# Casts of one batch's values cut into blocks of rows, and the order of all steps written anew, in a fused attention and highway kernel

## The chip, the core and the metric

The kernel runs on one core of a Trainium2 chip. A core has a matrix engine (TensorE, PE in the profile, with its weight loads as PEld), three engines for elementwise work (VectorE or DVE, ScalarE or ACT, GpSimd or POOL), and a fifth, SyncE or SP, whose queue issues nearly all DMAs here. They run at the same time and wait for each other through semaphores; each works off its own instructions in program order. The metric is the time of one execution on the device in microseconds.

## What is computed

An attention without a softmax over scores, and a highway layer over its result. Batch 8, 8 heads, 576 rows, 64 columns a head; all in float32 from and to memory.

```
q_s = exp(q) / sum over a head's columns          k_s = exp(k) / sum over the rows
kv  = k_s^T @ v            (64 x 64 for each batch and head)
x   = q_s @ kv             (4608 rows of 8 * 64 = 512)
H   = max(x @ w_h, 0)      T = sigmoid(x @ w_t + b_t)
out = T * H + (1 - T) * x
```

## The kernel before

The rows are worked off in 36 tiles of 128 rows. Two batches make nine tiles: four of the first, four of the second, one mixed. So tiles 0 to 3 and 4 to 7 belong to batches 0 and 1 and tile 8 to both; tiles 27 to 30, 31 to 34 and 35 belong to batches 6 and 7.

Nothing is scheduled by a compiler. The string ORDER (L16 to L63) lists some 700 steps, and the loop at L502 issues them one after the other. A step is named by its kind and its place, with an engine after a colon: `vc_1_2:A` casts slab 2 of batch 1's values on ACT. The order of the list is the order of each engine's own instructions, and so also of the DMA queue. Steps for a batch: `q`, `k`, `v` load (SP); `ek`, `eq` take the exponential into f16 (ACT); `vc` casts v into f16 (L258); `kv` is the product of k and v with an extra column of ones for the sums (PE, L264); `kr` and `kn` divide by the sums and keep the result (DVE); `qt` and `qc` turn q by TensorE and copy it out of PSUM; for batch 7 `qd` turns it by DMA. Steps for a tile: `xu` multiplies q with kv (PE), `rs` and `x` divide (DVE), `xt` and `xe` turn x and copy it (PE, then DVE or ACT), `mh` and `mt` are the products with the two weights (PE, L421 and L413, four of 512 columns each), `bw` puts the bias into the PSUM tile of mt (ACT), `th` is the tanh (ACT), `dd` and `uu` make the gated difference (DVE, or with `:P` two operations on POOL, "lifted", L451), `oo` adds x (POOL, L473), `st` stores (SP). `fill` are products of zeros that keep TensorE running in the first 15 us while the first loads arrive.

What ties the steps together beside the data are the buffers, which are used in turn:

- Loads of k, of v and of q have three buffers each; a load waits until the batch three before has been read.
- x in f16 has six buffers (`xp`): `x` of a tile waits for `oo` of the sixth tile before it in order.
- The outputs of two neighbouring tiles share one of seven buffers named o32 (the four halves of the weights pass through them first), so `oo` waits until the stores of the pair seven buffers before have landed. The mixed tiles and the last ones have three buffers of their own (o1).
- The products xu of a whole tile and kv share one PSUM tile (`ps_x`), so each waits until the one before has been read by DVE. The turned x has one PSUM tile, the turned q one, gate and H two each.
- d, u, tanh and the sums have three buffers each.

The cast is short:

```
def vc(e, b, c):
    n = 1 if b < 3 else 2
    copy = dict(A=nc.scalar.copy, D=nc.vector.tensor_copy, P=nc.gpsimd.tensor_copy)[e or "P"]
    copy(v16[b % NV][:, c:c + n, :, 0:D], T[f"v32{b}"][:, c:c + n].rearrange("p c (j d) -> p c j d", j=NJ))
```

A slab of batches 0 to 2 is 128 partitions by 9 blocks of 64, 576 elements a partition; without a letter the cast runs on POOL.

Of the kernel before, what the change touches and what calls it, by code (L numbers as in the profile page):

```python
# [16 lines left out]
setuppool q_0_0 v_0_0 fill_8 fill_8 b_32 b_0 eq_0_0 k_0_0 ek_0_0 qt_0_0 setupdve bsplit bp bc fill_8 ek_0_1 vc_0_0:D
v_0_1 vc_0_1 kv_0_0 kr_0_0 k_0_2 fill_8 ek_0_3 v_0_2 v_0_3 vc_0_2 qc_0_0 kn_0_0 xu_0_0 vc_0_3 ek_0_2 kv_0_1 kr_0_1
kn_0_1 q_0_4 fill_5 eq_0_1 eq_0_2 xu_1_0 rs_1_0 rs_0_0 x_1_0 x_0_0 fill_8 xt_1_0 xe_1_0:D qt_0_1 w_h_0 whd_1:P whd_0:P
whc_0:A qc_0_1 xt_0_0 xu_0_1 rs_0_1 x_0_1 bw_1 xe_0_0 xu_3_0 rs_3_0 x_3_0 qt_0_2 bw_0 w_h_2 whd_2:P whd_3:P whc_2:A  # L20
w_t_2 wtc_2:P xt_0_1 mh_0_0 xe_0_1:D xu_2_0 xt_3_0 xe_3_0 rs_2_0 w_t_0 wtc_0:P mh_1_0 q_1_0 mh_0_1 qc_0_2:A x_2_0
xt_2_0 dd_1 dd_0 k_1_2 eq_1_0 v_1_2 mt_1_0 th_1_0 uu_1_0 vc_1_3 oo_1_0 ek_1_2 ek_1_3 xe_2_0:D mt_0_1 mt_0_0 th_0_0
qt_1_0 qc_1_0 mh_3_0 bw_2 mt_2_0 vc_1_2:A kv_1_1 uu_0_0 oo_0_0 th_2_0 bw_3 mt_3_0 k_1_0 ek_1_1 ek_1_0 dd_3 kr_1_1
v_1_0 vc_1_0 vc_1_1:A kn_1_1 xu_5_1 th_3_0 rs_5_1 x_5_1 mh_2_0 dd_2 uu_2_0:P uu_3_0:P oo_2_0 oo_3_0 xt_5_1 xu_4_1
kv_1_0 kr_1_0 rs_4_1 bw_5 kn_1_0 xe_5_1 mt_5_1 x_4_1 q_1_4 eq_1_2 xu_5_0 rs_5_0 qt_1_2 qc_1_2 bw_4 xu_4_0 xu_8_0 x_5_0
eq_1_1 xt_5_0 qt_1_1 rs_4_0 x_4_0 mh_5_1 q_2_0 eq_2_0 k_2_2 rs_8_0 xe_5_0:D qc_1_1:A x_8_0 ek_2_3 xt_4_0 xt_4_1
xe_4_0:D xe_4_1:D mh_5_0 dd_5 mt_5_0 th_5_0 uu_5_0:P k_2_0 ek_2_1 bw_8:A ek_2_2 xu_6_0 rs_6_0 x_6_0 mt_4_1 xt_8_0
xe_8_0:D xu_6_1 rs_6_1 qt_2_0 x_6_1 xu_7_0 rs_7_0 x_7_0 mt_4_0 xt_6_0 xu_7_1 rs_7_1 xt_6_1 xe_6_0:D xe_6_1:D x_7_1
mt_8_0 ek_2_0 v_2_0 vc_2_0:D qc_2_0 mh_4_1 mh_4_0 xt_7_0 dd_4 xt_7_1 th_4_0 vc_2_1 kv_2_0 v_2_2 vc_2_3 vc_2_2:A kv_2_1
kr_2_1 mh_8_0 bw_6:A mh_6_1 th_8_0 mt_6_1 kr_2_0 oo_5_0 kn_2_1 uu_4_0:P kn_2_0 xu_9_0 dd_8 q_2_4 eq_2_2 eq_2_1 xe_7_1  # L30
uu_8_0:P oo_4_0 rs_9_0 x_9_0 mt_6_0 xe_7_0 qt_2_1 qc_2_1 th_6_0 mh_6_0 dd_6 mh_7_1 xt_9_0 xu_12_0 rs_12_0 x_12_0
uu_6_0:P oo_8_0 oo_6_0 xe_9_0:D mh_7_0 dd_7 bw_7:A mt_7_1 mt_7_0 xu_10_0 xt_12_0 mh_9_0 xe_12_0:D rs_10_0 q_3_0 x_10_0
eq_3_0 eq_3_1 qt_3_2 qc_3_2 dd_9 mh_12_0 xt_10_0 xe_10_0:D qt_3_1 qc_3_1 k_3_0 th_7_0 bw_10:A v_3_0 vc_3_0 xu_11_0
rs_11_0 bw_9:A mt_9_0 ek_3_0 ek_3_2 dd_12 vc_3_2:A x_11_0 qt_3_0 th_9_0 qc_3_0 uu_7_0:P oo_7_0 uu_9_0 mt_10_0 th_10_0
bw_12:A kv_3_0 qt_2_2 q_4_0 qc_2_2:A mh_10_0 eq_4_0:F kr_3_0 kn_3_0 xt_11_0 xe_11_0:D mt_12_0 dd_10 uu_10_0:P oo_9_0
oo_10_0 xu_14_0 rs_14_0 x_14_0 th_12_0 uu_12_0 oo_12_0 mh_11_0 qt_4_0 bw_11:A xu_13_0 rs_13_0 x_13_0 v_4_0 vc_4_0
xt_14_0 xe_14_0:D vc_4_2:A bw_14:A mt_11_0 th_11_0 xu_17_0 rs_17_0 x_17_0 qc_4_0:A xt_13_0 mh_14_0 dd_11 uu_11_0:P
oo_11_0 xu_15_0 rs_15_0 xe_13_0:D x_15_0 mt_14_0 dd_14 mh_13_0 xu_16_0 rs_16_0 x_16_0 bw_13:A xt_17_0 xe_17_0:D
mt_13_0 dd_13 k_4_0 ek_4_0 ek_4_2 q_4_9 kv_4_0 kr_4_0 kn_4_0 th_14_0 uu_14_0:P bw_17:A th_13_0 uu_13_0 xt_15_0 xe_15_0
qt_4_1 qc_4_1 mt_17_0 xu_18_0 rs_18_0 x_18_0 oo_14_0 q_5_0 eq_5_0 oo_13_0 v_5_0 vc_5_0 bw_15:A vc_5_2 mh_17_0 xt_16_0  # L40
xe_16_0:D dd_17 eq_4_2 eq_5_1 mt_15_0 th_15_0 xu_20_0 qt_4_2 k_5_0 rs_20_0 x_20_0 mh_15_0 th_17_0 uu_17_0:P oo_17_0
xt_18_0 mh_16_0 xu_19_0 dd_15 qc_4_2 xe_18_0:D rs_19_0 qt_5_0 qc_5_0 bw_16:A ek_5_0:F xt_20_0 x_19_0 q_6_0 xe_20_0:D
mt_16_0 th_16_0 bw_18:A qt_5_1 kv_5_0 eq_6_0:F dd_16 kr_5_0 kn_5_0 uu_16_0 bw_20:A xt_19_0 mh_18_0 qc_5_1:A st_1_0
st_1_1 mh_20_0 st_3_0 uu_15_0:P oo_15_0 xe_19_0:D xu_21_0 rs_21_0 x_21_0 oo_16_0 mt_18_0 th_18_0 k_6_0 st_3_1 v_6_0
mt_20_0 xu_22_0 dd_18 uu_18_0 oo_18_0 st_5_0 st_7_1 q_5_9 st_5_1 xt_21_0 rs_22_0 x_22_0 th_20_0 dd_20 uu_20_0:P
xe_21_0:D st_7_0 qt_6_0 mh_19_0 xu_23_0 rs_23_0 x_23_0 vc_6_2 dd_19 bw_19:A bw_21:A mt_19_0 ek_6_0 ek_6_2 mh_21_0
dd_21 xt_22_0 xe_22_0 xu_24_0 mt_21_0 mh_22_0 xt_23_0 rs_24_0 qc_6_0 x_24_0 vc_6_0:A kv_6_0 qt_6_1 th_19_0 uu_19_0:P
oo_20_0 q_6_9 dd_22 xe_23_0:D mh_23_0 kr_6_0 th_21_0 uu_21_0 oo_19_0 kn_6_0 bw_22:A mt_22_0 qc_6_1:A dd_23 xu_25_0
rs_25_0 x_25_0 eq_5_2 xt_24_0 qt_5_2 bw_23:A mt_23_0 th_22_0 oo_21_0 uu_22_0:P oo_22_0 qc_5_2:A xu_26_0 xe_24_0
rs_26_0 x_26_0 bw_24:A th_23_0 uu_23_0 xt_25_0 mh_24_0 dd_24 st_10_1 q_7_0 oo_23_0 v_7_0 st_10_0 vc_7_0 vc_7_2 k_7_0  # L50
mt_24_0 xe_25_0 eq_6_2 xu_27_0 qt_6_2 xt_26_0 mh_25_0 rs_27_0 x_27_0 xe_26_0:D xu_29_0 rs_29_0 bw_25:A mt_25_0 st_17_0
eq_7_0:F qd_7_0 qc_6_2:A dd_25 th_24_0 qd_7_1 x_29_0 xt_27_0 xe_27_0 uu_24_0 oo_24_0 mh_26_0 dd_26 xu_30_0 rs_30_0
th_25_0 x_30_0 st_12_0 uu_25_0:P mh_27_0 bw_27:A mt_27_0 st_14_1 dd_27 xt_30_0 xu_28_0 rs_28_0 q_7_9 st_12_1 bw_26:A
mt_26_0 st_14_0 st_23_0 st_16_0 st_16_1 xe_30_0:D mh_30_0 ek_7_0 oo_25_0 x_28_0 xt_28_0 xe_28_0:D ek_7_2 kv_7_0
xt_29_0 th_26_0 uu_26_0 oo_26_0 th_27_0 uu_27_0:P mh_28_0 bw_30:A mt_30_0 kr_7_0 kn_7_0 xu_31_0 st_21_0 bw_28:A
mt_28_0 dd_30 xe_29_0:D rs_31_0 dd_28 th_30_0 uu_30_0:P mh_29_0 x_31_0 xt_31_0 xe_31_0:D oo_27_0 oo_30_0 bw_29:A
xu_33_0 eq_7_2 th_28_0 rs_33_0 uu_28_0 mt_29_0 qt_7_2 bw_31:A mh_31_0 x_33_0 xt_33_0 xu_32_0 th_29_0 dd_29 rs_32_0
uu_29_0 qc_7_2:A oo_29_0 x_32_0 xe_33_0 mt_31_0 mh_33_0 xt_32_0 bw_33:A th_31_0 dd_31 st_8_0 st_19_0 st_26_0 xu_34_0
xe_32_0 uu_31_0 rs_34_0 mt_33_0 x_34_0 oo_28_0 st_28_0 st_30_0 oo_31_0 st_31_0 st_25_0 mh_32_0 xu_35_0 dd_33 xt_34_0
bw_32:A mt_32_0 th_33_0 uu_33_0:P oo_33_0 dd_32 xe_34_0:D mh_34_0 rs_35_0 x_35_0 xt_35_0 bw_34:A th_32_0 uu_32_0 dd_34  # L60
xe_35_0 mt_34_0 th_34_0 uu_34_0 oo_32_0 st_33_0 st_32_0 oo_34_0 st_34_0 bw_35_0 mh_35_0 dd_35 mt_35_0 th_35_0 uu_35_0
# [5 lines left out]
def kernel(  # L67
# [49 lines left out]
    spare = turned.rearrange("p a c d -> p (a c d)").bitcast(FP32)
    T = {}
# [136 lines left out]
        nc.scalar.activation(t[:, :, c:c + n].rearrange("p j c d -> p c j d"),  # L255
                             T[f"k32{b}"][:, c:c + n].rearrange("p c (j d) -> p c j d", j=NJ), AF.Exp)

    def vc(e, b, c):  # L258
        n = 1 if b < 3 else 2
        copy = dict(A=nc.scalar.copy, D=nc.vector.tensor_copy, P=nc.gpsimd.tensor_copy)[e or "P"]  # L260
        copy(v16[b % NV][:, c:c + n, :, 0:D], T[f"v32{b}"][:, c:c + n].rearrange("p c (j d) -> p c j d", j=NJ))  # L261
# [274 lines left out]
```

## Time and profile before

| | us |
|---|---|
| median of three runs (117.75 to 118.05) | 117.75 |
| the profiled execution | 117.78 |
| its span | 116.0 |
| TensorE busy | 109.2 |
| DVE, ACT, POOL busy | 93.7, 91.2, 90.9 |
| 40.58 MB moved, mean | 350 GB/s |

The profile is of one execution; times in it count from the start of its span, and 1.78 us of the execution lie outside of the span. Matmuls are pipelined and their ends are modelled, so what a product occupies is read from the distance of starts. A line of a timeline gives the start, the length, engine and line, operation, output and input, how many instructions were merged and, in brackets, the idle time ahead of it with what ended it.

### The profile page before, as it was taken

The numbers are of one execution on the slowest core, as the hardware profiler recorded it, in microseconds if no ns is written. First come the engines' busy times: TensorE is split into PE (matmuls) and PEld (weight loads), VectorE is DVE, ScalarE is ACT, GpSimd is POOL, SyncE is SP. The second block draws the span as 40 slices with busy tenths as digits, with TensorE's granted clock in tenths as the row PEclk, the third lists the DMA queues.
The fourth block names the chain that finished last, engine by engine and source line by source line (L and its number), as shares of the span: only waits on it lengthen the run. The fifth ranks groups of instructions, "written<-read, shape, count | busy, mean of one in ns | idle before, by whom it ended". The sixth has DMA issues, their size and how long they took to land.

```text
span 116.0 us, 3454 instructions
## 1 busy us (share of the span) xinstructions
PE 109.2 (94%) x1355; PEld 62.8 (54%) x1355; DVE 93.7 (81%) x231; ACT 91.2 (79%) x139; POOL 90.9 (78%) x103
## 2 busy tenths in 40 slices
...
PEclk9999999999999999999999999999999999999995
DMA  2999999999999999999999999999999999894965
GB/s 49 375 397 379 407 391 378 390 377 367 384 384 379 390 393 366 367 393 355 349 386 388 363 401 406 391 384 332 370 398 376 148 276 394 343 364 166 401 257 181
DMA packets 24755, 40.58 MB, mean 350 GB/s; under 512 B 5410, under 2 KB 12834, under 8 KB 24740
## 3 DMA queue, kind: packets, MB, share of 16 engines
...
q8 instruction: 10, 0.16, 0.6%
q10 hardware_dynamic: 148, 0.14, 0.4%
...
## 4 chain that ended last, share of the span: by engine, by line
PE 54%; POOL 26%; DVE 6%; issue 6%; DMA 2%; ACT 1%; POOLq 1%; ACTq 0%
POOL o L473 14%; PE gps L421 14%; PE tps L413 13%; PE turned L168 10%; POOL u L453 6%; PE kv L271 4%; PE xu L363 4%; PE turned L386 4%; PE qps L326 3%; POOL g L452 3%; DMA out_dram<-o 2%; POOL v L261 2%; DVE x L378 2%; DVE d L441 2%; DVE xT L393 1%
## 5 line engine op out<-in xcount | busy, mean ns | idle before, releaser
L473 POOL TENSOR_TENSOR o<-u,x 128x512 f32<-128x512 f16 (+1 forms) x36 | 40.5, 1142 | 2.1 <-DVE u L455 1.2
L413 PE MATMUL tps<-w16t,xT 128*128 128x512 f16 (+1 forms) x148 | 37.2, 373 | 0.0
L421 PE MATMUL gps<-w16h,xT 128*128 128x512 f16 x144 | 36.9, 379 | 0.0
L378 DVE TENSOR_TENSOR x<-xu,rs 128x512 f16<-128x512 f32 (+1 forms) x41 | 25.5, 624 | 2.5 <-POOL g L452 0.5
L441 DVE SCALAR_TENSOR_TENSOR d<-x,gps 128x512 f16<-128x512 f16 x36 | 24.1, 677 | 0.5 <-PE gps L421 0.4
L453 POOL TENSOR_TENSOR u<-g,d 128x512 f16<-128x512 f16 x19 | 21.9, 1155 | 1.6
L261 POOL CAST v<-v 128x576 f16<-128x576 f32 (+1 forms) x14 | 12.6, 906 | 11.4 <-DMA v<-in_v_dram 11.3
L255 ACT ACTIVATE ek<-k 128x576 f16<-128x576 f32 (+2 forms) x21 | 18.8, 930 | 2.6 <-DMA k<-in_k_dram 2.5
L413 PEld LDWEIGHTS <-xT 128*128 128x128 f16 x148 | 13.4, 98 | 10.7 <-ACT xT L393 0.2
L421 PEld LDWEIGHTS <-xT 128*128 128x128 f16 x144 | 12.9, 98 | 10.9 <-DVE xT L393 0.8
L401 ACT COPY tps<-ball 128x512 f32<-128x512 f32 x29 | 16.8, 590 | 2.4 <-DVE u L455 2.1
L363 PE MATMUL xu<-kvb,eq 128*128 128x130 f16 (+1 forms) x160 | 15.4, 225 | 0.3 <-DVE x L378 0.2
L363 PEld LDWEIGHTS <-eq 128*128 128x128 f16 (+1 forms) x160 | 10.4, 100 | 8.4 <-DVE x L378 3.6
L386 PE MATMUL turned<-idh,x 128*128 128x128 f16 x144 | 14.5, 220 | 0.1
L309 ACT ACTIVATE qe<-q 128x1024 f16<-128x1024 f32 (+2 forms) x11 | 9.5, 896 | 5.3 <-DMA q<-in_q_dram 5.3
L386 PEld LDWEIGHTS <-x 128*128 128x128 f16 x144 | 10.2, 98 | 6.1 <-DVE x L378 1.6
L455 DVE SCALAR_TENSOR_TENSOR u<-tps,d 128x512 f16<-128x512 f32 (+1 forms) x17 | 11.4, 668 | 2.5 <-ACT tps L437 1.9
L168 PE MATMUL turned<-blank 128*128 128x512 f16 x45 | 12.1, 420 | 1.3 <-POOL blank L150 1.3
L452 POOL TENSOR_SCALAR g<-th 128x512 f16<-128x512 f16 x19 | 11.7, 618 | 1.2 <-DVE x L378 1.2
L435 ACT ACTIVATE th<-tps 128x512 f16<-128x512 f32 x19 | 11.2, 592 | 1.7 <-PE tps L413 1.6
L393 DVE COPY xT<-turned 128x512 f16<-128x512 f16 (+1 forms) x28 | 10.6, 384 | 2.3 <-PE turned L386 2.3
L437 ACT ACTIVATE tps<-tps 128x512 f32<-128x512 f32 (+1 forms) x18 | 10.0, 556 | 2.4 <-PE tps L413 2.4
...
## 6 DMA issues: line engine op xcount, KB each, us to landing
...
```

What stands on the lines that cost most here:

```text
L168: nc.tensor.matmul(spare, blank[:, 0:P], blank, start=True, stop=True, skip_group_check=True)
L255: nc.scalar.activation(t[:, :, c:c + n].rearrange("p j c d -> p c j d"), T[f"k32{b}"][:, c:c + n].rearrange("p c (j d) -> p c j d", j=NJ), ...
L363: nc.tensor.matmul(dst, turned_q(b, jp, n), kvb[b % NKV][:, hh, kk], start=True, stop=True, skip_group_check=True)
L378: nc.vector.tensor_mul(t[:, k0:k1], sums(i, k)[:, :, :, 0:64], T[f"rs{i}_{k}"][:, 0:k1 - k0].unsqueeze(3).to_broadcast([P, k1 - k0, 4, D]))
L386: nc.tensor.matmul(t[:, n], T[f"x{i}"][:, n0 + n % 2:n0 + 2 * P:2], idh, is_transpose=True, start=True, stop=True, skip_group_check=True)
L401: nc.scalar.copy(t[:, cs], ball[:, cs])
L413: nc.tensor.matmul(T[gate(i, k)][:, cs], T[f"xT{i}"][:, n], w16["t"][:, n, cs], start=False, stop=(n == parts[-1] and not first), skip_gro ...
L421: nc.tensor.matmul(t, T[f"xT{i}"][:, n], w16["h"][:, n], start=(first and n == parts[0]), stop=(n == parts[-1] and not (first and len(part ...
L441: nc.vector.scalar_tensor_tensor(t, T[f"x{i}"], -0.5, T[f"gps{i}"], op0=ALU.mult, op1=ALU.max)
L452: nc.gpsimd.tensor_scalar(g, T[f"th{i}"], 1.0, 1.0, op0=ALU.add, op1=ALU.mult)
L453: nc.gpsimd.tensor_mul(t, g, T[f"d{i}"])
L473: eng.tensor_add(t[:, cs], T[f"u{i}_{h}"][:, cs], T[f"x{i}"][:, cs])
```

## The change

`vc` gets a fourth argument: part 0 is the first five of a slab's nine blocks, part 1 the other four. The list uses it for two slabs of batch 1, those that are loaded last. Each is cast by two operations, in the list one on POOL and one on ACT. The whole list of steps is written anew: many steps change place, some their engine, and some pairs of operations are one now or the reverse. Cut to the steps that the text speaks of:

```diff
-... v_1_2 mt_1_0 th_1_0 uu_1_0 vc_1_3 oo_1_0 ek_1_2 ek_1_3 ... vc_1_2:A kv_1_1 ...
-v_1_0 vc_1_0 vc_1_1:A kn_1_1 xu_5_1 th_3_0 ... kv_1_0 kr_1_0 ...
+... v_1_2 th_0_0 vc_1_2 uu_0_0 oo_0_0 ek_1_3 th_1_0 qc_1_0 uu_1_0 ek_1_2 vc_1_3:A ...
+... v_1_0 vc_1_1_1 vc_1_0_0 bw_3 mt_3_0 th_3_0 uu_3_0:P vc_1_0_1:A kv_1_1 mh_2_0 bw_2 vc_1_1_0:A ... kv_1_0 ...
...
-... k_5_0 ... q_6_0 ... st_1_0 st_1_1 st_3_0 k_6_0 st_3_1 v_6_0 st_5_0 st_7_1 q_5_9 st_5_1 st_7_0 q_6_9
-st_10_1 q_7_0 v_7_0 st_10_0 k_7_0 st_17_0 qd_7_0 qd_7_1 st_12_0 st_14_1 q_7_9 st_12_1 ...
+... st_3_0 k_5_0 q_6_0 st_1_0 st_1_1 st_3_1 k_6_0 q_5_9 q_7_9 v_6_0 st_5_0 st_7_0 st_5_1 st_7_1
+q_7_0 v_7_0 k_7_0 st_10_0 st_10_1 qd_7_0 st_12_0 qd_7_1 q_6_9 st_12_1 ...
...
-... qt_6_2 ... eq_7_0:F qc_6_2:A th_24_0 xe_27_0 th_25_0 bw_27:A bw_26:A ek_7_0 ek_7_2 th_26_0 ...
+... th_22_0 eq_7_0:F bw_25:A th_24_0 vc_7_2:A bw_26:A th_25_0 vc_7_0:A bw_27:A ek_7_0:F th_26_0 ...
...
-    def vc(e, b, c):
+    def vc(e, b, c, part=None):
         n = 1 if b < 3 else 2
+        js = slice(0, NJ) if part is None else slice(5 * part, 5 + 4 * part)
         copy = dict(A=nc.scalar.copy, D=nc.vector.tensor_copy, P=nc.gpsimd.tensor_copy)[e or "P"]
-        copy(v16[b % NV][:, c:c + n, :, 0:D], T[f"v32{b}"][:, c:c + n].rearrange("p c (j d) -> p c j d", j=NJ))
+        copy(v16[b % NV][:, c:c + n, js, 0:D], T[f"v32{b}"][:, c:c + n].rearrange("p c (j d) -> p c j d", j=NJ)[:, :, js])
```

The first part of the lists is in the order of all steps, the second only the DMA queue's, the third only ACT's. Further counts of the new list: 44 fills for 45; 18 lifted gates for 19; `eq_3`, `ek_4`, `ek_6` and `ek_7` are one operation each, where they were two, and `eq_4` two where it was one; of batch 0's four casts three are on DVE and one on POOL, where it was the reverse; both casts of batch 7 move from POOL to ACT. On TensorE `mh_30` stands behind `kv_7_0`, where it stood ahead of it.

More of the change, by code (lines that the diff above doesn't have):

```diff
@@ L16 @@
 ORDER = """
[L17 to L61, printed above, removed]
@@ L62 @@
-oo_35_0 bw_35_1 mt_35_1 st_35_0 th_35_1 uu_35_1 oo_35_1:D st_35_1:A
+setuppool b_0 q_0_0 v_0_3 v_0_2 b_32 fill_8 fill_8 v_0_0 k_0_2 v_0_1 eq_0_0 setupdve vc_0_0 fill_8 qt_0_0 fill_6
+bsplit vc_0_2:D ek_0_3 vc_0_3:D ek_0_2 kv_0_1 qc_0_0 kr_0_1 k_0_0 fill_8 vc_0_1:D kn_0_1 ek_0_0 ek_0_1 kv_0_0 kr_0_0
+kn_0_0 xu_0_1 q_0_4 eq_0_2 qt_0_2 bp qc_0_2 xu_0_0 xu_1_0 eq_0_1 qt_0_1 fill_6 rs_0_1 x_0_1 rs_1_0 xt_0_1 rs_0_0 x_0_0
+xt_0_0 x_1_0 bc bw_0 xe_0_1:D qc_0_1:A xu_2_0 w_h_0 rs_2_0 x_2_0 w_h_2 whd_1:P whd_0:P whc_0:A xe_0_0 whd_2:P whd_3:P
@@ new lines @@
+whc_2:A w_t_2 wtc_2:P bw_1 xt_1_0 xe_1_0:D mh_0_0 xu_3_0 xt_2_0 mh_0_1 mh_1_0 w_t_0 wtc_0:P xe_2_0 rs_3_0 x_3_0 xt_3_0
+mt_0_1 mt_0_0 mt_1_0 q_1_0 eq_1_0 qt_1_0 dd_1 k_1_2 dd_0 xe_3_0:D v_1_2 th_0_0 vc_1_2 uu_0_0 oo_0_0 ek_1_3 th_1_0
+qc_1_0 uu_1_0 ek_1_2 vc_1_3:A mh_3_0 dd_3 oo_1_0 k_1_0 ek_1_1 ek_1_0 v_1_0 vc_1_1_1 vc_1_0_0 bw_3 mt_3_0 th_3_0
+uu_3_0:P vc_1_0_1:A kv_1_1 mh_2_0 bw_2 vc_1_1_0:A kr_1_1 kn_1_1 xu_5_1 mt_2_0 th_2_0 dd_2 uu_2_0:P bw_5 xu_4_1 rs_5_1
+x_5_1 xt_5_1 xe_5_1 rs_4_1 x_4_1 kv_1_0 kr_1_0 kn_1_0 q_1_4 eq_1_2 mt_5_1 qt_1_2 qc_1_2 bw_4 xu_5_0 rs_5_0 xu_4_0
@@ new lines @@
+rs_4_0 x_5_0 x_4_0 xu_8_0 eq_1_1 qt_1_1 xt_5_0 xe_5_0:D rs_8_0 k_2_0 ek_2_0 mh_5_1 xt_4_0 xt_4_1 qc_1_1:A mh_5_0
+xe_4_1 oo_3_0 xu_6_1 mt_5_0 x_8_0 xe_4_0:D dd_5 rs_6_1 x_6_1 mt_4_1 xt_8_0 xu_6_0 rs_6_0 x_6_0 xe_8_0:D k_2_2 ek_2_2
+ek_2_3 mt_4_0 th_5_0 bw_8:A ek_2_1 mh_4_1 mh_4_0 dd_4 xt_6_1 th_4_0 oo_2_0 xe_6_1 v_2_0 xu_7_0 rs_7_0 x_7_0 vc_2_1
+mt_8_0 bw_6:A vc_2_0 xu_7_1 rs_7_1 x_7_1 kv_2_0 v_2_2 vc_2_3 vc_2_2 kv_2_1 kr_2_0 kn_2_0 kr_2_1 xt_6_0 mh_8_0 q_2_0
+eq_2_0 kn_2_1 qt_2_0 qc_2_0 xe_6_0 q_2_4 th_8_0 xt_7_1 mt_6_1 mt_6_0 eq_2_1 eq_2_2 bw_9:A uu_5_0:P oo_5_0 uu_4_0:P
@@ new lines @@
+dd_8 uu_8_0:P oo_4_0 th_6_0 xt_7_0 xu_9_0 rs_9_0 xe_7_1:D x_9_0 xe_7_0:D mh_6_1 qt_2_1 qc_2_1 mh_6_0 dd_6 mh_7_1
+xt_9_0 xe_9_0:D bw_7:A mt_7_1 mt_7_0 oo_8_0 uu_6_0:P qt_2_2 xu_12_0 q_3_0 eq_3_0:F qc_2_2 mt_9_0 rs_12_0 x_12_0 mh_7_0
+dd_7 qt_3_2 k_3_0 xu_10_0 xt_12_0 rs_10_0 xe_12_0:D v_3_0 vc_3_0 mh_9_0 qc_3_2 th_7_0 x_10_0 uu_7_0 mh_12_0 th_9_0
+xu_11_0 rs_11_0 oo_6_0 xt_10_0 xe_10_0:D ek_3_0 ek_3_2 qt_3_0 bw_12:A x_11_0 mt_12_0 xt_11_0 dd_12 dd_9 qc_3_0 oo_7_0
+uu_9_0:P oo_9_0 vc_3_2:A kv_3_0 kr_3_0 mh_10_0 bw_10:A mt_10_0 kn_3_0 xu_14_0 th_12_0 uu_12_0 oo_12_0 xe_11_0 mh_11_0
@@ new lines @@
+qt_3_1 rs_14_0 x_14_0 dd_10 xu_13_0 rs_13_0 x_13_0 q_4_0 eq_4_0 eq_4_1 xt_14_0 bw_11:A mt_11_0 th_10_0 uu_10_0 xu_17_0
+rs_17_0 x_17_0 qc_3_1:A qt_4_0 xe_14_0 mh_14_0 qc_4_0 xt_17_0 th_11_0 xu_15_0 dd_11 rs_15_0 x_15_0 bw_14:A mt_14_0
+bw_17:A v_4_0 vc_4_2 vc_4_0 oo_10_0 xe_17_0 uu_11_0:P dd_14 oo_11_0 k_4_0 q_4_9 eq_4_2 mt_17_0 xu_16_0 th_14_0 uu_14_0
+rs_16_0 q_5_0 xt_13_0 xe_13_0:D x_16_0 ek_4_0:F th_17_0 bw_13:A mh_17_0 dd_17 uu_17_0:P v_5_0 qt_4_1 qc_4_1:A oo_14_0
+vc_5_2 oo_17_0 mh_13_0 dd_13 kv_4_0 st_3_0 xt_15_0 xe_15_0 mt_13_0 kr_4_0 k_5_0 kn_4_0 qt_4_2 xt_16_0 xe_16_0:D
@@ new lines @@
+xu_18_0 rs_18_0 qc_4_2 x_18_0 eq_5_0 th_13_0 mh_15_0 dd_15 bw_15:A mh_16_0 uu_13_0 oo_13_0 xu_20_0 xt_18_0 vc_5_0
+q_6_0 st_1_0 mt_15_0 rs_20_0 x_20_0 st_1_1 eq_5_1 xe_18_0:D qt_5_1 qc_5_1 bw_16:A mt_16_0 st_3_1 k_6_0 xu_19_0 rs_19_0
+q_5_9 x_19_0 q_7_9 qt_5_0 qc_5_0 v_6_0 st_5_0 st_7_0 st_5_1 th_15_0 uu_15_0:P oo_15_0 st_7_1 q_7_0 xt_20_0 xe_20_0:D
+mh_18_0 ek_5_0:F kv_5_0 th_16_0 xt_19_0 bw_18:A dd_16 uu_16_0:P mt_18_0 oo_16_0 bw_20:A mt_20_0 eq_6_0:F kr_5_0
+xe_19_0:D kn_5_0 dd_18 xu_21_0 rs_21_0 x_21_0 v_7_0 mh_20_0 th_18_0 uu_18_0 qt_6_1 k_7_0 st_10_0 dd_20 th_20_0
@@ new lines @@
+uu_20_0:P oo_18_0 xt_21_0 bw_19:A xu_22_0 rs_22_0 x_22_0 mh_19_0 xe_21_0:D mt_19_0 dd_19 st_10_1 xu_23_0 rs_23_0
+xt_22_0 ek_6_0:F mh_21_0 xe_22_0:D mh_22_0 x_23_0 vc_6_0 th_19_0 uu_19_0 oo_19_0 dd_21 oo_20_0 xu_24_0 rs_24_0 xt_23_0
+xe_23_0:D bw_21:A mt_21_0 qc_6_1:A eq_5_2 qt_5_2 x_24_0 qc_5_2 dd_22 mh_23_0 dd_23 vc_6_2:A kv_6_0 kr_6_0 kn_6_0
+qt_6_0 eq_7_2 th_21_0 uu_21_0:P bw_23:A mt_23_0 bw_22:A xu_25_0 rs_25_0 x_25_0 oo_21_0 qc_6_0:A xt_24_0 xe_24_0:D
+th_23_0 bw_24:A mt_22_0 th_22_0 xu_26_0 rs_26_0 uu_23_0:P eq_7_0:F qd_7_0 st_12_0 x_26_0 qd_7_1 q_6_9 qt_7_2 xt_25_0
```

12 lines of the change are left out of this document (added).

## The prediction

> **What bounds the kernel now.** I read the page first, then the stretches, then engine by engine the timeline around the last attention product. The page's head, with its DMA digits:
>
> ```profile
> span 116.0 us, 3454 instructions
> PE 109.2 (94%) x1355; PEld 62.8 (54%) x1355; DVE 93.7 (81%) x231; ACT 91.2 (79%) x139; POOL 90.9 (78%) x103
> ...
> PEclk9999999999999999999999999999999999999995
> DMA  2999999999999999999999999999999999894965
> ```
>
> TensorE is busy 94% of the span at full clock, and the DMA engines are full until slice 31 (about 90 us). The busy time by stretch (columns: start and end, length, then PE, PEld, DVE, ACT, POOL, clock, DMA share, GB/s):
>
> ```profile
> 30.00:60.00 30.00, 29.90 (x452) 18.47 (x451) 28.08 (x71) 29.22 (x43) 28.60 (x30) 1.00 1.07 377
> 60.00:90.00 30.00, 29.81 (x382) 18.00 (x379) 26.87 (x60) 28.11 (x42) 27.96 (x29) 1.00 1.05 381
> 90.00:111.00 21.00, 21.00 (x220) 11.68 (x217) 17.91 (x38) 14.86 (x27) 19.26 (x20) 1.00 0.93 302
> ```
>
> All four engines run nearly full, and TensorE has no hole. The timeline of TensorE around the last k-v product (step kv_7, L271):
>
> ```profile
> 93.07 1.03 PE L421 MATMUL gps<-w16h,xT 128*128 128x512 f16 x4
> 93.94 0.39 PE L386 MATMUL turned<-idh,x 128*128 128x128 f16 x4
> 94.25 0.78 PE L271 MATMUL kv<-v,ek 64*64 64x65 f16 x72
> 94.96 0.40 PE L386 MATMUL turned<-idh,x 128*128 128x128 f16 x4
> 95.20 1.03 PE L421 MATMUL gps<-w16h,xT 128*128 128x512 f16 x4
> ```
>
> Starts tell what a step occupies: four 512-column products 0.866 us, four transposes 0.225, the xu of a full tile 0.235, kv of a batch 0.71 to 0.76, eight turns of q 0.45. The list's TensorE steps at these prices make 103.9 us; TensorE starts at 1.3 and its last step leaves at 111.05, so 5.8 us are lost, 1.5 of them in the first slow fills and about 2 between 30 us and the end. Such a kernel has little to win and much to lose: any wait of TensorE after 30 us adds itself to the end. What gates kv_7 (ACT, POOL, DVE and SP timelines):
>
> ```profile
> 91.85 2.22 ACT L255 ACTIVATE ek<-k 128x1152 f16<-128x1152 f32 x2 [0.64 <-DMA k<-in_k_dram]
> ```
> ```profile
> 88.52 2.24 POOL L261 CAST v<-v 128x1152 f16<-128x1152 f32 x2
> 90.72 1.16 POOL L473 TENSOR_TENSOR o<-u,x 128x512 f32<-128x512 f16 x1
> ```
> ```profile
> 92.82 0.68 DVE L378 TENSOR_TENSOR x<-xu,rs 128x512 f16<-128x512 f32 x1
> ```
> ```profile
> 78.25 0.57 SPq L184 DMA_DIRECT2D v<-in_v_dram  x1
> 78.88 0.83 SPq L493 DMA_DIRECT2D out_dram<-o  x1
> 79.77 0.59 SPq L184 DMA_DIRECT2D k<-in_k_dram  x1
> 80.45 0.71 SPq L481 DMA_DIRECT2D out_dram<-o  x1
> 88.33 3.80 SPq L342 DMA_TRANSPOSE eq<-qe  x2
> ```
>
> The k of batch 7 is issued at 79.77 and released at 91.85: twelve us of queue lie ahead of it. The POOL sum at 90.72 is tile 24's (oo_24); its output takes the slot that tiles 9 and 10 hold until their stores land, the last of which (78.88) is in front of that k. x of tile 28 (92.82) takes the buffer that oo_24 gives back.
>
> **The change, part by part.** The split itself: the list gives batch 1's last two slabs to POOL (two operations) and ACT (two), none to DVE. A 128x576 cast takes 666 ns on POOL and 665 on ACT, a 128x1152 one 1146 and 1154, so 0.84 ns an element and 0.18 fixed: 320 elements 0.45, 256 elements 0.40. Each engine gets 0.85 for 0.67, 0.19 more. Before, both casts start when v lands and the product follows:
>
> ```profile
> 26.57 0.67 ACT L261 CAST v<-v 128x576 f16<-128x576 f32 x1 [0.29 <-DMA v<-in_v_dram]
> ```
> ```profile
> 26.60 0.66 POOL L261 CAST v<-v 128x576 f16<-128x576 f32 x1 [0.16 <-DMA v<-in_v_dram]
> ```
>
> After, the loads ahead of that v are the same bytes; the casts end near 27.45, kv_1_0 moves from 27.32 to 27.5. The 0.15 is absorbed, since the turn of q behind it waits in both kernels for q's rest, released at 28.37. Taken alone, 0 to 0.2 us.
>
> The rest is the new list. TensorE's steps are the same but for one fill (0.22 less). POOL gets 18 lifted gates for 19 (each 0.62 + 1.16 there, 0.68 on DVE) and fewer casts: 2.7 us less. ACT gets 1.0 more, DVE 0.9 more; copies of xT and q change sides. None of these sums bounds: laid end to end from 28 us, start to start, they finish by 103 (DVE), 102 (ACT) and 106 (POOL), TensorE by 109. What can cost is order, so I walked the new list by hand with these starts, taking a DMA's release at the byte count where the trace has it. Until 30 us the loads decide, and their bytes up to q's rest of batch 1 are the same. I give a k-v product's start plus the TensorE work from it on, before and after: kv_1_1 24.41 + 83.87 = 108.28 against 24.45 + 83.87 = 108.32; kv_3 48.20 + 61.44 = 109.64 against 48.05 + 61.55 = 109.60; kv_4 110.15 against 60.25 + 49.77 = 110.02; kv_6 79.36 + 31.24 = 110.60 against 79.75 + 30.26 = 110.01. Inside, after waits 0.5 at kv_1_1 (vc_1_3 stands behind four ACT operations), 0.3 at the second half of kv_2 (four casts in a row on POOL), 0.3 behind kv_6 (two dd ahead of kn_6 on DVE). So 0.6 us ahead at 80 us; error of the walk about 0.5 either way.
>
> At kv_7 three things meet. (a) TensorE arrives at 92.95. (b) ACT: k_7 has two stores fewer ahead (0.52 MB; 32.9 MB by 91.85 is near 0.375 MB a us, so 1.4 us): released at 90.45. But ACT starts eq_7 at 84.2 to 84.8 and then does 1.85, 0.54, 0.55, 1.06, 0.54, 0.55, 1.06, 0.54 and 2.05 up to the end of ek_7: 92.95 to 93.55. (c) The stores of tiles 9 and 10 are moved behind k_7. Ahead of the last of them stand now 32.9 MB, what before stood up to k_7, so it lands at about 91.85. POOL reaches oo_24 by 89.7 and must wait. oo_24 ends 1.12 later, x_28 needs 0.05 + 0.69 more, kv_7 shares xu's PSUM tile with x_28: start plus 1.95. With 91.85 kv_7 starts at 93.8. A store may land later than a load at the same place. The nearest row is the chain of waits' end, a 256 KB store on an almost empty queue:
>
> ```profile
> 109.17 2.79 DMA out_dram<-o
> ```
>
> 0.7 us is its data at 0.375 MB a us, so up to 2.1 us come on top: 91.85 to 93.95, kv_7 at 93.8 to 95.9. The load of k stands at the very same byte and shows the queue's lag already, so I stay near it: 92.0, kv_7 at 93.95.
>
> The Trainium skill (DMA: Bandwidth & Descriptors, section on the anatomy of one DMA) puts most of a fixed 2 us into the receipt from the target memory and calls HBM the heaviest. By that the store would come at the upper end and the sum be near 120.3; the row of 2.79 agrees with it for a lone store, and no row shows it inside a full queue.
>
> Sum: before, TensorE leaves kv_7 behind at 94.25 and ends 16.8 later, at 111.05. After, one product (mh_30, 0.866) stands behind kv_7 that stood before it: 17.67. 93.95 + 17.67 = 111.6, 0.55 later. The tail (last tanh, gate, sum, store) is the same steps in the same order and adds the same 4.9 to 116.0. 117.78, the profiled execution's time, of which 1.78 lie around the span, + 0.55 = 118.3; the median shown is 117.75, so nothing has to be shifted.
>
> **The rivals.** Not slower: the point that decides is kv_7's start of 93.4 (94.25 less 0.87). If the store's landing does not hold POOL (it lands by 90.4, as a faster queue ahead would make it), kv_7 starts with TensorE at 92.95 to 93.3, the end is 110.6 to 111.0, and most of what was won on the way stays: 117.3 with TensorE's own arrival. For it speaks that DMA digits were full and a smaller backlog is possible; against it ACT's own 93.0 to 93.55.
>
> Much slower: the late slot hits twice. The stores of tiles 0 and 1 now come after k_5 and q_6 and one store; oo_15 reaches its slot at 69.1 and finds it at 70.5 to 71. POOL has about 1.5 us of slack there by my walk; if that is gone, x_22 and the tiles after it move, and kv_7's wait comes on top at its upper end: 119.5 to 120.3.3.
>
> No change: TensorE catches up. If its steps could run closer than they do, a lost us would be regained and 117.8 stay. The rows are against it: in full stretches four products start each 0.86. The Trainium skill (TensorE: Matmul & The Clock Gate, section Back-to-back issue gap) gives some 131 ns for a 512-column product in a sustained stream; here it is 216, so the trace disagrees.
>
> The split does nothing it was made for: it runs on two engines, and all four pieces must be there before kv_1_0's products, so at best it is neutral; that gives the forecast's sum unchanged, since kv_1 is not where it decides.
>
> **How the numbers follow.** A change within 0.3% (0.35 us) can't be told from none. Forecast 118.3, own range 117.9 to 119.2: 0.48. Faster, 117.3: 0.25. Much slower, 119.5 to 120.3: 0.14. Catching up or cancelling, 117.8: 0.13. Of the forecast's 0.48 some 0.07 lie within 0.3%. So faster 0.25, same 0.20, slower 0.55. The range leaves out a tenth on each side: 117.1 to 120.3, from kv_7 without any wait less some error of the walk up to a store at its latest.
>
> **What would show it.** In the profile after: POOL idle ahead of an o at about 90 to 92, released by a DMA of out_dram; kv of batch 7 at 93.5 to 95 with a gap of TensorE ahead of it of 0.5 to 2 us; the rest of the stream as dense as now; kv_6 near 79.7; POOL's sum at 2.5 us less. I am wrong if POOL runs through at 90 us, if TensorE has waits of over 0.5 us anywhere between 30 and 85 us, or if the start (first gps near 17) has moved by over 0.5.

## The result, and the profile after

The changed kernel takes 118.94 us in the median of seven runs (118.30 to 119.50); the kernel before took 117.98 in seven runs beside it. The ratio is 1.0068, with a 95% interval of 1.0040 to 1.0097: slower by about 0.8 us. A later series gave 1.0065 (1.0048 to 1.0082). The profiled execution took 118.51 us with a span of 116.7, 0.73 more than the one before.

The page's head after, with the digits of TensorE, its clock and the DMA engines over 40 slices:

```profile
span 116.7 us, 3459 instructions
PE 108.7 (93%) x1354; PEld 62.3 (53%) x1354; DVE 94.4 (81%) x234; ACT 92.1 (79%) x136; POOL 88.3 (76%) x101
...
PE   5999999999999999999999999999999779999930
...
PEclk9999999999999999999999999999999999999995
DMA  3999999999999999999999999999999797996474
```

Before, TensorE's row had a nine in every slice from the second to the thirty-eighth. Now two sevens stand at 90 to 96 us. The clock row is the same. The same three stretches as before (start and end, length, then PE, PEld, DVE, ACT, POOL, clock, DMA share, GB/s):

```profile
30.00:60.00 30.00, 29.97 (x388) 18.08 (x386) 27.89 (x69) 29.23 (x44) 29.14 (x31) 1.00 1.07 375
60.00:90.00 30.00, 29.99 (x449) 18.37 (x449) 27.00 (x65) 28.95 (x39) 28.36 (x29) 1.00 1.10 376
90.00:111.00 21.00, 19.77 (x205) 10.88 (x204) 17.27 (x36) 14.21 (x24) 16.85 (x17) 1.00 0.85 291
```

Up to 90 us TensorE is as dense as it was, and in the last stretch it lacks 1.2 us. The timeline of TensorE shows the hole, ahead of the last k-v product:

```profile
91.76 1.03 PE L414 MATMUL tps<-w16t,xT 128*128 128x512 f16 x4
94.02 0.77 PE L272 MATMUL kv<-v,ek 64*64 64x65 f16 x72 [1.23 <-ACT tps L402]
94.72 0.40 PE L387 MATMUL turned<-idh,x 128*128 128x128 f16 x4
```

The four products at 91.76 occupy TensorE for 0.866, so it is free at 92.63 and starts kv_7 1.39 later. Before, the distance from its arrival (transposes at 93.94, plus 0.225) to 94.25 was 0.09. The name in the bracket, a bias copy on ACT that ends at 93.90, is only the event that came last: that copy writes the PSUM of a gate, which kv_7 doesn't use. In a second profile of this kernel the bracket names x of tile 28 on DVE instead (1.27 us). What kv_7 needs is read from the other timelines, of ACT, POOL and DVE:

```profile
90.31 2.12 ACT L255 ACTIVATE ek<-k 128x2304 f16<-128x2304 f32 x1
```
```profile
91.99 2.26 POOL L474 TENSOR_TENSOR o<-u,x 128x512 f32<-128x512 f16 x2 [1.77 <-DMA out_dram<-o]
```
```profile
93.18 0.69 DVE L379 TENSOR_TENSOR x<-xu,rs 128x512 f16<-128x512 f32 x1 [1.24 <-POOL o L474]
```

The exponential of k ends at 92.44 and has no wait ahead of it. POOL comes to the sum of tile 24 (oo_24) at 90.22 and waits 1.77 us for a DMA out of an output buffer, where it ran at 90.72 before without a wait. x of tile 28 waits 1.24 us for that sum and ends at 93.87; kv_7 follows 0.15 later. In the queue, the load of batch 7's k now goes out first and the stores of tiles 9 and 10 behind it:

```profile
77.69 0.49 SPq L184 DMA_DIRECT2D k<-in_k_dram  x1
78.37 2.92 SPq L494 DMA_DIRECT2D out_dram<-o  x2
```

An account of the 0.64 us by which the last product starts later (111.25 against 110.61): at kv_6 the new list is ahead by 0.69 (start plus the TensorE work that is left: 79.65 + 30.26 = 109.91 against 79.36 + 31.24 = 110.60). The gap at kv_7 is 1.30 longer (1.39 against 0.09). 1.30 less 0.69 is 0.61.

In what follows, the traces are compared by the distance from the start of kv_1_0 to the start of the last product, since the time up to kv_1_0 (27.3 to 28.1 us) scatters between executions of lists that are the same up to there. What a change adds ahead of kv_1_0 is not in it, so for the split a second distance is given, from the start of the first cast of the two slabs. The first distance is 83.29 before and 83.72 and 83.80 in two profiles of the changed kernel.

### The profile page after: what moved, and what is told of

The parts are those of the page before. It is cut to its first block, busy times and chain, and to the rows that moved or that the text cites. A ratio compares the mean times of both kernels' runs of the same rounds, so it can differ in the third digit from the quotient of the medians.

```text
span 116.7 us, 3459 instructions
## 1 busy us (share of the span) xinstructions
PE 108.7 (93%) x1354; PEld 62.3 (53%) x1354; DVE 94.4 (81%) x234; ACT 92.1 (79%) x136; POOL 88.3 (76%) x101
## 4 chain that ended last, share of the span: by engine, by line
PE 61%; DMA 21%; ACT 11%; DVE 2%; issue 2%; DVEq 0%
PE tps L414 20%; PE gps L422 20%; DMA k<-in_k_dram 11%; DMA q<-in_q_dram 10%; PE turned L387 6%; PE xu L364 6%; PE kv L272 4%; PE qps L327 3%; PE qps L322 2%; ACT v L262 2%; ACT ek L255 2%; ACT th L436 2%; ACT tps L402 2%; ACT tps L438 2%; ACT qe L305 1%
## 5 line engine op out<-in xcount | busy, mean ns | idle before, releaser
L414 PE MATMUL tps<-w16t,xT 128*128 128x512 f16 (+1 forms) x148 | 36.7, 373 | 0.3 <-ACT xT L394 0.3
L454 POOL TENSOR_TENSOR u<-g,d 128x512 f16<-128x512 f16 x18 | 20.8, 1158 | 2.1 <-DVE d L442 0.6
L262 POOL CAST v<-v 128x576 f16<-128x576 f32 (+3 forms) x14 | 11.5, 842 | 8.9 <-DMA v<-in_v_dram 8.3
L364 PE MATMUL xu<-kvb,eq 128*128 128x130 f16 (+1 forms) x160 | 14.9, 224 | 0.0
L456 DVE SCALAR_TENSOR_TENSOR u<-tps,d 128x512 f16<-128x512 f32 (+1 forms) x18 | 12.1, 671 | 2.2 <-ACT tps L438 1.8
L438 ACT ACTIVATE tps<-tps 128x512 f32<-128x512 f32 (+1 forms) x19 | 10.6, 557 | 3.0 <-PE tps L414 2.8
L453 POOL TENSOR_SCALAR g<-th 128x512 f16<-128x512 f16 x18 | 11.2, 622 | 0.3 <-ACT th L436 0.3
L436 ACT ACTIVATE th<-tps 128x512 f16<-128x512 f32 x18 | 10.7, 592 | 0.7 <-PE tps L414 0.6
```

The costliest lines, as they stand in the source:

```text
L262: copy(v16[b % NV][:, c:c + n, js, 0:D], T[f"v32{b}"][:, c:c + n].rearrange("p c (j d) -> p c j d", j=NJ)[:, :, js])
L364: nc.tensor.matmul(dst, turned_q(b, jp, n), kvb[b % NKV][:, hh, kk], start=True, stop=True, skip_group_check=True)
L414: nc.tensor.matmul(T[gate(i, k)][:, cs], T[f"xT{i}"][:, n], w16["t"][:, n, cs], start=False, stop=(n == parts[-1] and not first), skip_gro ...
L436: nc.scalar.activation(T[f"th{i}"], src, AF.Tanh, scale=0.5)
L454: nc.gpsimd.tensor_mul(t, g, T[f"d{i}"])
```

## The experiments

The theory was that one chain decides: late stores, so a late output slot, so a late sum of tile 24, so a late x buffer, so a late x of tile 28, so a late kv_7, with nothing left on TensorE to fill the gap. The rivals were that ACT's exponential holds kv_7 as well, that the split itself costs the time, that the place of the stores costs it in any list, and that the new list is slower throughout.

**Another output slot.**

```diff
-    op = pool("op", 7)
+    op = pool("op", 8)
```

> The kernel after the change with eight shared output buffers instead of seven; nothing else is moved. Theory (the store of tiles 9 and 10 holds the slot of oo_24): oo_24 now takes a slot whose stores landed near 80 us, so POOL's 1.77 us of idle ahead of it at 90.23 to 92.00 go, x of tile 28 starts near 92.0 instead of 93.18, and kv of batch 7 starts when ek_7 (ends 92.44) and x_28 (92.7) are done: 92.7 to 92.9 instead of 94.02. TensorE ends 1.1 to 1.3 us earlier, the time falls to 0.99 of after, that is about 117.6, at or under before. Rival (k of batch 7, or ACT's eq_7 to ek_7 chain, is what gates): POOL's idle goes, kv_7 stays at 93.5 or later, the time stays within 0.3 us of after. Rival (many small waits of the new list): no more than 0.3 us either.

117.89 us, ratio to the kernel before 0.9982 (0.9967 to 0.9998). The sum of tile 24 runs at 90.73 with 0.08 of idle time, x of tile 28 at 92.57, and kv_7 starts 1.13 after the start of the four products ahead of it, where it was 2.26. The distance is 82.64, 1.08 less than in the changed kernel. The first link of the chain, cut alone, gives back the whole loss and a little more.

**Another buffer for x.**

```diff
-    xp = pool("xp", 6)
+    xp = pool("xp", 7)
```

> The kernel after the change with seven buffers for x in f16 instead of six; the output slots stay seven. This takes away only the second link: x of tile 28 no longer waits for oo_24, which still waits for the store. Theory: POOL still idles about 1.8 us ahead of oo_24 (start near 92.0), but x_28 starts near 92.0 and kv_7 near 92.8; the time falls by 1.0 to 1.3 us, as with eight output slots. Rival (POOL's own lateness costs, through the last sums and stores): POOL is as late as in after, so the time falls by 0.3 us at most.

117.66 us, ratio 0.9948 (0.9927 to 0.9968), distance 82.77. The timelines of POOL, DVE and TensorE:

```profile
91.94 2.26 POOL L474 TENSOR_TENSOR o<-u,x 128x512 f32<-128x512 f16 x2 [1.82 <-DMA out_dram<-o]
```
```profile
91.99 0.69 DVE L379 TENSOR_TENSOR x<-xu,rs 128x512 f16<-128x512 f32 x1
```
```profile
91.70 1.03 PE L414 MATMUL tps<-w16t,xT 128*128 128x512 f16 x4
92.83 0.92 PE L272 MATMUL kv<-v,ek 64*64 64x65 f16 x72
```

POOL waits as long as it did, to 91.94. But x no longer needs the buffer that this sum gives back; it runs at 91.99, and kv_7 starts at 92.83, 1.2 earlier. So POOL's 1.8 us of idle time cost nothing in themselves: in the changed kernel they cost through the buffer. The same executions show that ACT does not hold kv_7 at 94 either, its exponential ending at 92.39. What is left at kv_7, 0.26, is DVE's way from xu of tile 28 to its x, since kv shares their PSUM tile.

**The stores back ahead of k.**

```diff
-... st_7_1 q_7_0 ... v_7_0 ... k_7_0 st_10_0 ... st_10_1 ...
+... st_7_1 st_10_1 q_7_0 ... v_7_0 ... st_10_0 k_7_0 ...
```

> The kernel after the change with the two stores of tiles 9 and 10 at the places they had before: one ahead of q_7, one ahead of k_7; the DMA queue alone is changed. Theory: the wait of oo_24 goes (the later store lands near 89.5), but k_7 lands 0.7 MB a us's worth of 0.52 MB later, 1.4 us, so ek_7, one operation of 2.1 us, would start near 91.8 and end near 93.9: kv_7 at 94.0, no earlier than in after. The gate is exchanged, the time stays within 0.4 us of after. Rival (the stores' place alone is the cause, k_7 has room): kv_7 near 92.8 and 1.1 us off the time.

(The 1.4 us expected for k are 0.52 MB at 0.375 MB a us.) 118.69 us, ratio 1.0050 (1.0025 to 1.0074), distance 83.64. The sum of tile 24 runs at 90.68 with no wait, but now ACT waits for k:

```profile
92.00 2.12 ACT L255 ACTIVATE ek<-k 128x2304 f16<-128x2304 f32 x1 [1.06 <-DMA k<-in_k_dram]
```

The exponential ends at 94.12 and kv_7 starts at 94.17. The order of these three transfers only decides which of the two gates is late: whichever stands last is released at 91.9 to 92.2, the store for POOL or the k for ACT. That also measures the point that the prediction left open, whether a store lands later than a load at the same place in a full queue. In these traces it doesn't: 92.00 for the load here, 91.99 for the store there, and 91.90 to 92.17 in five more profiles of kernels that have the stores last.

**The stores later still.**

```diff
-... k_7_0 st_10_0 ... st_10_1 ... qd_7_0 st_12_0 ...
+... k_7_0 ... qd_7_0 st_12_0 st_10_0 st_10_1 ...
```

> The kernel after the change with the two stores of tiles 9 and 10 put still later in the DMA queue: behind the first turn of q by DMA and the first store of tiles 11 and 12. About 0.5 MB more stand ahead of the second, 0.262 MB of a store and the turn. Theory: oo_24 starts 0.7 to 2 us later than 92.0, and x_28, kv_7 and the end follow one for one: the time rises by 0.7 to 2 us over after. Rival (the wait at oo_24 is covered by something else that is as late): no change within 0.3 us.

120.90 us, ratio 1.0239 (1.0190 to 1.0289). The sum of tile 24 starts at 93.60, 1.61 later than in the changed kernel, x of tile 28 at 94.78 and kv_7 at 95.62. Up to there the chain moved as a whole, one for one. But the last product starts 3.28 later, at 114.53. The rest is in the stretches of one us behind kv_7 (columns as above):

```profile
96.00:97.00 1.00, 1.00 (x56) 0.71 (x42) 1.00 (x3) 0.00 (x0) 0.89 (x2) 0.96 0.99 393
98.00:99.00 1.00, 1.00 (x4) 0.36 (x3) 0.29 (x1) 0.14 (x1) 0.93 (x1) 0.50 0.03 12
100.00:101.00 1.00, 1.00 (x7) 0.50 (x5) 0.59 (x2) 0.97 (x2) 0.40 (x1) 0.84 0.99 379
```

TensorE stood idle for 3.00 us ahead of kv_7, counted from starts like the 1.39 above (2.84 by the profile's modelled ends), and from 97 to 100 us its granted clock is 0.50. By the 0.96 and the 0.84 of the stretches at both sides it was halved from 96.92 to 100.32. Its timeline there:

```profile
96.56 1.56 PE L422 MATMUL gps<-w16h,xT 128*128 128x512 f16 x4
97.91 1.91 PE L414 MATMUL tps<-w16t,xT 128*128 128x512 f16 x4
99.62 0.65 PE L364 MATMUL xu<-kvb,eq 128*128 128x130 f16 x4
100.06 1.16 PE L422 MATMUL gps<-w16h,xT 128*128 128x512 f16 x4
```

The four products at 97.91 occupy 1.71 us where 0.866 is usual. The four steps shown take 4.50, from 96.56 to the next step's start at 101.06, where three times 0.866 and 0.235 make 2.83: 1.67 more, which is what comes on top of the 1.61. The six runs bear it out: three with a mean clock of 0.975 to 0.984 (the traced one is among them) took 121.41 to 121.76, three at 1.000 took 120.03 to 120.38. So this longer wait costs some 1.4 us more than the changed kernel's where the clock stays up (120.26 in the middle of the three, against 118.9), and about 1.5 more again where it drops (121.74).

**The same late stores with eight slots.** This kernel is the one just shown with the eighth output slot.

> The changed kernel with the two stores behind a further DMA turn and two loads, as in the slow version that had a TensorE stall of 2.8 us and then half the clock for some 3 us, but with eight output slots, so that the sum of tile 24 needs another pair's stores. Theory: the late stores cost only through the slot and the idle TensorE; without the wait no stall ahead of kv_7 over 0.3 us, clock at 1.00 from 92 to 102 us, and a time of 0.997 to 1.002 of the kernel before. Rival: the moved stores cost by themselves, through the DMA queue and the turns of q behind them: 1.01 or more even so.

(Between k and these two stores stand one DMA turn and one store, as in the run before, and no loads.) 117.66 us, ratio 0.9969 (0.9946 to 0.9992), distance 82.93. The sum runs at 90.40, kv_7 at 93.17 with 0.10 of idle time, and the clock is 1.00 from 92 to 102 us. So the place of the stores costs nothing by itself that the times show, through the queue or the turns of q behind them (with the stores in their earlier place eight slots gave 0.9982, in another series); all of the 3 us in the kernel above came by way of the slot.

**The old list with the stores behind k.**

```diff
-... st_10_1 q_7_0 oo_23_0 v_7_0 st_10_0 vc_7_0 vc_7_2 k_7_0 mt_24_0 ...
+... q_7_0 oo_23_0 v_7_0 vc_7_0 vc_7_2 k_7_0 st_10_0 st_10_1 mt_24_0 ...
```

> The kernel before with the stores of tiles 9 and 10 moved behind the load of batch 7's k, as the new list has them, and nothing else. Theory: k is released some 1.4 us earlier (near 90.4), the sum of tile 24 waits for the last store until about 92 where it ran at 90.7, and x of tile 28 follows at 93.2; but mh_30 still stands ahead of kv_7, and TensorE comes there at 94.1, so kv_7 starts within 0.3 us of where it did, and the time is within 0.3 us of the kernel before. Rival: the stores' place alone makes the loss, in any list: 0.5 to 0.8 us slower.

118.07 us against 118.02, ratio 1.0011 (0.9998 to 1.0024), distance 83.39. POOL and TensorE:

```profile
91.99 1.15 POOL L473 TENSOR_TENSOR o<-u,x 128x512 f32<-128x512 f16 x1 [1.26 <-DMA out_dram<-o]
```
```profile
94.26 0.78 PE L271 MATMUL kv<-v,ek 64*64 64x65 f16 x72
```

Here is the whole chain of the changed kernel, with the sum at 91.99 and x of tile 28 at 93.18 as there, in a list where it costs nothing measurable: mh_30 stands ahead of kv_7, and TensorE isn't there before 94.2. The late slot alone is not the loss. It takes a TensorE that arrives early.

**Work put into the gap.**

```diff
-... xu_28_0 rs_28_0 x_28_0 xt_30_0 xe_30_0:D mt_27_0 th_26_0 dd_26 ... kv_7_0 xt_28_0 mh_30_0 ...
+... xu_28_0 rs_28_0 xt_30_0 xe_30_0:D dd_26 x_28_0 mt_27_0 th_26_0 ... mh_30_0 kv_7_0 xt_28_0 ...
```

> The changed kernel with the product mh_30 (0.87 us) ahead of kv_7, as it stood before, and with the turn, the copy and dd_26 that it needs ahead of x_28 on DVE; the wait for the stores is left as it is. Theory: the slot comes free at the same time, kv_7 starts near 94.0 to 94.5, but TensorE has spent 0.87 us of its 1.4 us of stall on mh_30, so that it waits 0.4 to 0.6 us there and the work left behind kv_7 is 0.87 us less: the end comes 0.5 to 0.9 us earlier than in the changed kernel, 118.0 to 118.4 where that has 118.9. Rival, the stall is not what sets the end (something behind kv_7 does, as q's second half or a DMA turn): no gain, 118.7 to 119.1.

118.14 us against 118.25 of the kernel before in its series, ratio 1.0013 (0.9990 to 1.0036), distance 83.25, 0.47 less than in the changed kernel:

```profile
92.88 1.03 PE L422 MATMUL gps<-w16h,xT 128*128 128x512 f16 x4
94.01 0.77 PE L272 MATMUL kv<-v,ek 64*64 64x65 f16 x72
```

kv_7 starts where it did, at 94.01, since the slot is as late as it was. But TensorE spends 0.866 of the gap on a product that it owed anyway. The gap that is left is 0.26, less than the expected 0.4 to 0.6, for TensorE came there 0.26 later in this execution.

**The split undone in the new list.** Both late slabs are cast whole, at the places of their first pieces.

```diff
-... v_1_0 vc_1_1_1 vc_1_0_0 bw_3 ... uu_3_0:P vc_1_0_1:A kv_1_1 mh_2_0 bw_2 vc_1_1_0:A kr_1_1 ...
+... v_1_0 vc_1_0 bw_3 ... uu_3_0:P kv_1_1 mh_2_0 bw_2 vc_1_1:A kr_1_1 ...
```

> The changed kernel with whole casts of the two late slabs of batch 1 (one on POOL, one on ACT) at the places of the first pieces, the rest of the new list kept. Theory: the split costs nothing and brings nothing, since the wait of tile 24's sum for the stores of tiles 9 and 10 decides: time within 0.3 us of the changed kernel (118.6 to 119.2 where that has 118.9), kv_1_0 starts within 0.2 us of 27.5, TensorE's stall of some 1.4 us ahead of kv_7 and POOL's idle of 1.8 us ahead of the sum at 92.0 stay. Rival, the split itself costs the time: POOL and ACT are 0.4 us less busy, and the kernel returns to 118.0 to 118.3.

118.50 us, ratio 1.0023 (1.0006 to 1.0040), distance 83.66. POOL's wait (1.49, to 91.90) stays, and so does a gap at kv_7, of 0.98, since TensorE came there 0.32 later in this execution; kv_7 starts at 93.93. So the main loss is not the split's, but the ratio lies below the 1.0065 and 1.0068 of the changed kernel, which came from two other series.

**The changed kernel once more,** in a third series, for that reason.

> The changed kernel once more, as it is, since whole casts in its list gave 1.0023 of the kernel before where it had given 1.0068 in another series. Theory, the split costs nothing: the traces put 83.7 us between kv_1_0 and the last product in both, so the ratio comes out at 1.002 to 1.005, level with the whole casts within their intervals. Rival, the split costs some 0.4 us: 1.006 to 1.008 again.

118.73 us, ratio 1.0065 (1.0048 to 1.0082), distance 83.80. The rival's figure came out. By the ratios, whole casts are worth 0.42% (0.5 us, about 0.2 to 0.8); by the times 0.23 us (118.73 less 118.50), since the kernel before was at 118.25 in the one series and 118.02 in the other; by the distances 0.06 to 0.14. The traces show nothing behind the split that could cost as much. In the new list all that follows waits for the store: the last product starts 19.26 us after the sum of tile 24 in all three profiles, and the sum starts 65.31 and 65.39 after the first cast with pieces, 65.35 with whole casts.

**The split alone in the old list.**

```diff
-v_1_0 vc_1_0 vc_1_1:A kn_1_1 ...
+v_1_0 vc_1_1_1 vc_1_0_0 vc_1_0_1:A vc_1_1_0:A kn_1_1 ...
```

> The kernel before with the four pieces alone, everything else as before (two pieces on POOL, two on ACT, where the whole casts stood). Theory: POOL and ACT get 0.19 us each at 27 us, kv_1_0 moves from 27.32 to about 27.5, and the turn of q, which waits for its load, takes that up: time within 0.3 us of the kernel before, no wait of TensorE ahead of kv_7. Rival, the split costs as much as the whole change: 0.6 to 0.9 us slower than before.

118.36 us against 118.25, ratio 1.0011 (0.9992 to 1.0029), distance 83.18 (83.29 before): by the ratio between a gain of 0.1 us and a loss of 0.35. From the start of the first cast, so with what the pieces add ahead of kv_1_0, it is 84.05 to the last product, and 84.03 before. What the pieces take is plain. The two on POOL and the two on ACT in the changed kernel:

```profile
26.68 0.80 POOL L262 CAST v<-v 128x256 f16<-128x256 f32 x2 [0.18 <-DMA v<-in_v_dram]
```
```profile
26.72 0.75 ACT L262 CAST v<-v 128x256 f16<-128x256 f32 x2
```

0.80 and 0.75, against 0.66 for a whole one. In the new list ACT's next tanh and copy of xT slide by about 0.1, and TensorE waits 0.28 for that copy at 28.28, a wait that is not there with whole casts. The wait for q's rest behind it takes that up: the eight turns of q start 1.50 after q's release with pieces and with whole casts alike. So the traces show no cost of the split in either list, and its ratio in the old list allows at most 0.35 us. That the changed kernel and whole casts differ by 0.2 to 0.8 us in their ratios is not explained; they did not run in one series.

**The old list with seven x buffers.** The control for the best edit so far.

> The kernel before with seven buffers for x in f16 instead of six, its own list kept: the control for the same edit on the new list. Theory: in the old list x of tile 28 follows the end of tile 24's sum too (92.82 after 91.87), but TensorE has no stall there and ek_7 holds kv_7 until 94.1, so nothing is to be won: within 0.3 us of the kernel before. Rival, the seventh buffer helps any list, by waits of x elsewhere: 0.4 to 0.8 us faster, so that the new list with seven buffers owes its gain to the buffer and not to its order.

117.83 us against 118.25, ratio 0.9965 (0.9950 to 0.9980), distance 82.81. That was not expected to gain. Most of the gain (0.31 of the 0.48 by the distances) is not at kv_7 but at 76 us. DVE in the kernel before, and with seven buffers:

```profile
76.06 0.69 DVE L378 TENSOR_TENSOR x<-xu,rs 128x512 f16<-128x512 f32 x1 [0.47 <-POOL g L452]
```
```profile
75.79 0.69 DVE L378 TENSOR_TENSOR x<-xu,rs 128x512 f16<-128x512 f32 x1
```

x of tile 23 waited 0.47 us for POOL in the kernel before; a few DVE operations later x of tile 24 was late too, and kv_6, which waits for it, started 0.31 late (11.24 us after kv_5, against 10.93). So the new list with seven buffers (0.9948) owes its gain over the kernel before to the buffer as much as to its order: the two lists, each with seven, are 0.9948 and 0.9965 with intervals that overlap.

**Both buffers.** The changed kernel with seven x buffers and eight output slots.

> The changed kernel with seven x buffers and eight output slots together. Theory: with seven x buffers kv_7 follows TensorE's own order with no stall, so the eighth slot takes POOL's idle 1.8 us away and nothing else: 0.994 to 0.996 of the kernel before, as seven x buffers alone. Rival: POOL's late sums hold later tiles as well, and the slot gives another 0.3 to 0.5 us: 0.990 to 0.992.

117.49 us, ratio 0.9957 (0.9940 to 0.9974), distance 82.67. POOL's wait is gone (the sum runs at 90.25), and the time is that of seven x buffers alone within the intervals. Seven x buffers, with seven slots or eight, are about 0.5% faster than the kernel before.

## Why the prediction was right

It said 118.3, slower by 0.55 us, from 117.1 to 120.3. Measured: 118.94 in the median, 118.51 in the profiled execution, which is 0.73 more than its counterpart before; slower by about 0.8 in the ratio. By its own steps:

**The split, 0 to 0.2 us.** Two pieces were to take 0.85 and took 0.80 and 0.75; kv_1_0 was to start at 27.5 and started at 27.53. The turn of q behind it took it up, starting at 29.89 (29.99 before). The traces show no cost, and the split alone in the old list allows at most 0.35 us by its ratio, so the upper end of 0.2 is borne out by the traces and not settled by the times.

**The sums of the engines.** POOL 2.7 less, ACT 1.0 and DVE 0.9 more were forecast; 2.6 less, 0.9 and 0.7 more were measured. None of them bounds, as said.

**The walk to kv_6.** kv_3 at 48.05, kv_4 at 60.25 and kv_6 at 79.75 were forecast; 47.97, 60.06 and 79.65 came, a lead of 0.69 for 0.6. Of the three waits inside, 0.5, 0.3 and 0.3, only half of the first shows: TensorE, free at 24.07, starts kv_1_1 at 24.32. At the second half of kv_2 and behind kv_6 there is none; between 25 and 92 us the profile has no idle time of TensorE of over 0.3 us in one piece. Right in the sum, wrong in these places: some 0.5 us of waits ahead of kv_6 that did not come were nearly made up for by other steps, which took longer than the walk had them. That the two cancel is luck, and which steps took longer isn't worked out.

**The three at kv_7.** (a) TensorE was to arrive at 92.95 and came at 92.63. (b) The exponential of k was to end at 92.95 to 93.55 and ended at 92.44, since ACT began eq_7 at 83.70 and not at 84.2 to 84.8. So the argument that ACT would hold kv_7 anyhow was wrong by 0.5 to 1.1 us; it decided nothing, as the runs with another buffer show by kv_7's start at 92.83. (c) POOL was to reach the sum by 89.7 and came at 90.22; it had to wait even so. The store was to release it at 92.0 and did at 91.99; kv_7 was put at 93.95 and started at 94.02.

**The choice at the store's landing,** the widest of the bounds, 91.85 to 93.95, was made for the nearest row, a load at the same byte of the queue, and held to 0.2 us in every kernel that had the store there. The Trainium skill's rule of the receipt (DMA: Bandwidth & Descriptors, the anatomy of one DMA), by which the sum was near 120.3, would have the store some 2 us behind. In this full queue a store and a load at one place were released at 91.99 and 92.00. That section of the Trainium skill is on DMAs that GpSimd issues, and these are SyncE's.

**Behind kv_7.** 0.87 more TensorE work was forecast: the last product starts 17.23 after kv_7, where it was 16.36.

**The rest of the sum.** Unrounded the sum gives 0.57. To it come 0.07 on the way from the store to kv_7 (put at 1.95 from the sum's start, measured 2.02) and 0.10 behind the last product (5.49 to the end of the span, 5.39 before), which make the 0.73 of the profiled pair. The rest of the 0.64 between 118.3 and 118.94 lies between executions: the medians of seven lie 0.20 above the profiled one before and 0.43 above it after.

**The rivals.** Not slower, 117.3 "with TensorE's own arrival": that arrival is what the seventh x buffer and the eighth slot produce, at 0.9948 to 0.9982 of the kernel before, 117.4 to 117.8 of 117.98. Much slower through oo_15: that sum does wait for its slot, 0.34 us, to 70.14, and the slack there was enough. Catching up: no, four products start 0.866 apart wherever TensorE is full. The break-even point was put at a kv_7 of 93.4; the changed kernel with its start at 94.02 lost 0.64, which puts it at 93.4.
